# Attention into MoE on one core: a load goes ahead of another, and the third query chunk changes its score, turn and value paths

## The chip, the core and the metric

The kernel runs on one core of a Trainium2 chip. The metric is the device time of one execution in microseconds (us); lower is better. Before the change the median of three runs is 624.77 us.

The engines named below: TensorE (PE: matrix products; its weight loads, PEld, run beside it), VectorE (DVE), ScalarE (ACT), GpSimd (POOL) and SyncE (SP, which issues most transfers). PE writes into eight PSUM banks of 128 x 512 float32; ACT and DVE read them out.

## What is computed

Attention with a causal window of 128 and 4 sink positions, for 4 batches, 8 heads, 768 positions, head size 64, then a feed-forward layer (512 to 2048 to 512) with a leaky activation per column:

```python
keep = is_sink | in_window                  # pos < n_sink, or 0 <= q - k < window
scores = np.where(keep, scale * q @ k.T, -1e9)
a = softmax(scores); x = a @ v              # x: (3072, 512), heads side by side
h = x @ w_in
g = np.maximum(h, 0.0) + alpha * np.minimum(h, 0.0)
return g @ w_out
```

Inputs are float32; the feed-forward weights arrive as float64. To keep float32 accuracy the kernel splits a factor into a high and a low part of the format fp32r and adds three products (high x high, high x low, low x high), or it multiplies float32 directly.

## The kernel before

**Tiling.** The 3072 tokens are 12 chunks `c` of 256 queries, three to a batch (`CPB` = 3). For a chunk, attention makes x (512 features as 4 blocks of 128, high part `xh` and low part `xl`); then for each of 16 weight blocks `f` of 128 hidden columns `gemm1` makes h (12 matmuls of 256 columns, line 984), ACT and DVE make g with its two parts (L993, L995, L999, L1000), and `gemm2` adds into two output banks (6 matmuls of 512 columns, L1037, L1039, L1040). From chunk 3 on some blocks serve two chunks at once.

**Attention of a chunk.** A unit is one head `h` and one half `u` of the queries. Its steps: scores on PE into a bank; the mask, the scaling and the row maximum on DVE (L662); exp with the row sum on ACT (L668); weights turned so that keys lie on partitions; products with v; x written out by ACT and DVE. The sinks' part is collected apart (`sink_step`) and multiplied with the sink rows of v (`vs`).

There are three ways in which chunks do this:
- Chunks 0 and 1 (`SPLIT`): `load_head` brings two heads in one transfer, head `h` in partitions 0 to 63 and head `h+1` in 64 to 127. The scores of both are float32 matmuls on half the rows each, with nothing prepared (L637). PE turns the weights (L687, L688), ACT copies them into `comb` tiles (L692), and the row sums divide after the value product (`av_split`, L882 to L906).
- Chunk 2: each head is loaded twice over the partitions; ACT and DVE make the high and low parts (`prep_head`, L608 to L612); two fp32r matmuls of 128 rows for a unit (L647, L648). DVE divides (L697 to L709), PE turns (L786), DVE multiplies with the two triangle masks `tri` (L790), and `av_two` does the value product in two halves of four heads (L859 for the sinks, L838).
- Chunks 3 to 11 (`c >= PAIRED`): scores as in chunk 2. The weights are turned by a 32 x 32 transpose on DVE (L800) and transfers to DRAM and back (`swap`, L803, L807); DVE multiplies with masks (`swapped`, L821, L824), and `av_four` does all eight heads with 64 x 64 quarters of PE (L944 for the sinks, then L938 twice with a drain between).

**Weights.** A block is loaded (L415), its float64 words are made into float32 by two DVE steps (L427, L429), its high part is cast by ACT (L435) and its low part subtracted by DVE (L438).

**The order.** The program isn't issued as written. `Plan` collects operations with an engine, an estimated cost, and what they read and write; `draw` simulates them once in Python and places on each engine, as it comes free, the waiting operation of the lowest rank among those that could start soonest. PE operations are ranked as they were written; others take the rank of their first consumer. The order so found is fixed. Where PE would idle in the first 60 us of the plan, `issue` puts in matmuls of no use on an idle bank (L1224, `fill`). Values of a kind (tiles or banks) are given out in the order in which they were asked for. SP's queue holds its transfers in this order; the first ones are ranked by hand with `then(...)` (lines 532 to 545): parameters, head pair 0, weight block 0, head pair 2, head pair 4, sink rows, head pair 6, v, weight blocks 1 to 3.

**Where chunk 2 stands.** The feed-forward work of chunks 0 and 1 is a list of 32 slots (`work`, lines 1161 to 1184). Attention of chunk 1 is put at slot 0, that of chunk 2 is spread over the last `LATE` = 11 slots; `convert(f + 2)` keeps the weight conversion two blocks ahead. At the end `judge` works out whether the inputs fit this program (limits on window, sinks, weights and scores); five of its DVE steps (L1141 to L1145) need only the parameters and can run at the start.

## Time and profile before

| | |
|---|---|
| median of 3 runs | 624.77 us (624.73 to 625.24) |
| profiled execution | 624.71 us |
| its span, first to last instruction | 623.2 us |
| outside the span | 1.5 us |
| busy: PE, DVE, ACT, POOL | 615.2, 508.8, 367.0, 34.6 us |
| granted TensorE clock | 1.00 of full speed throughout |

The busy time of PE holds matmuls of no use, and pipelined matmuls overlap in it, so 99% is not 99% useful. The chain of waits gives each matmul the time that it adds to the one before it, and is the view by which PE's work is costed here.

### The profile page before, as it was taken

What the parts mean: (1) busy time and instruction counts of PE and PEld (TensorE: products, weight loads), DVE (VectorE), ACT (ScalarE), POOL (GpSimd) and SP (SyncE); (2) the same over time, 40 slices, a digit from 0 to 9 for tenths busy, and PEclk for the clock granted to TensorE, in tenths of its full rate; (3) what the DMA queues carried; (4) which work ended last, traced back from release to release, by engine and by line L of the source; (5) the groups of instructions that cost most, each with busy time, mean ns of one, the idle gap of its engine ahead of it and who ended that gap; (6) DMA issues with size and microseconds to landing.
All of it is one profiled execution on the core that took longest, in us unless ns stands there. A gap on an engine that the chain in (4) does not pass through costs nothing.

```text
span 623.2 us, 13103 instructions
## 1 busy us (share of the span) xinstructions
PE 615.2 (99%) x4594; PEld 547.4 (88%) x4596; DVE 508.8 (82%) x1637; ACT 367.0 (59%) x963; POOL 34.6 (6%) x116
## 2 busy tenths in 40 slices
PE   8999999999999999999999999999999999999997
PEld 4678999989999999998988888898898898898896
DVE  7999999979999989989689789879879969933232
ACT  6887558748567367365366266266366456369232
POOL 3110000001000000010000000010000000000000
PEclk9999999999999999999999999999999999999999
DMA  8777812235544354544534444344344343310001
GB/s 313 273 280 265 290 55 65 94 97 170 157 128 162 115 160 129 174 129 130 160 102 128 124 138 128 109 149 144 107 129 137 102 153 104 111 36 0 1 36 37
DMA packets 64039, 82.89 MB, mean 133 GB/s; under 512 B 9824, under 2 KB 45152, under 8 KB 63968
## 3 DMA queue, kind: packets, MB, share of 16 engines
q1 hardware_dynamic: 60416, 69.04, 35.3%
q10 hardware_dynamic: 3552, 12.97, 5.7%
q8 instruction: 37, 0.61, 0.4%
q14 instruction: 34, 0.28, 0.1%
HBM read 65.05 MB, written 16.94 MB: 132 GB/s over the span
## 4 chain that ended last, share of the span: by engine, by line
PE 95%; DVE 2%; ACT 1%; issue 1%; DMA 0%; ACTq 0%
PE bank L984 40%; PE bank L1039 13%; PE bank L1037 13%; PE bank L1040 13%; PE bank L938 4%; PE bank L647 3%; PE bank L648 3%; PE bank L838 1%; PE bank L637 1%; PE bank L944 1%; PE bank L687 1%; ACT pt L668 1%; PE bank L688 0%; DVE w L438 0%; PE bank L1224 0%
## 5 line engine op out<-in xcount | busy, mean ns | idle before, releaser
L984 PE MATMUL bank<-xh,w 128*128 128x256 f32 (+1 forms) x1136 | 263.7, 314 | 0.5 <-DVE g L995 0.5
L984 PEld LDWEIGHTS bank<-xh,w 128*128 128x128 f32 x1136 | 192.8, 191 | 12.8 <-DVE g L995 1.0
L984 PE MATMUL bank<-xl,w 128*128 128x256 f32 (+1 forms) x568 | 177.2, 312 | 0.0
L1039 PE MATMUL bank<-w,gh 128*128 128x512 f32 x380 | 144.5, 380 | 0.0
L1040 PE MATMUL bank<-w,gh 128*128 128x512 f32 x380 | 144.2, 379 | 0.0
L993 ACT ACTIVATE g<-bank,param 128x256 f32<-128x256 f32 (+1 forms) x142 | 77.7, 548 | 102.7 <-PE bank L984 102.4
L1037 PE MATMUL bank<-w,gl 128*128 128x512 f32 x380 | 113.5, 381 | 0.0
L984 PEld LDWEIGHTS bank<-xl,w 128*128 128x128 f32 x568 | 108.5, 191 | 5.2
L999 ACT CAST gh<-g 128x256 fp32r<-128x256 f32 (+1 forms) x142 | 67.5, 479 | 67.0 <-DVE g L995 66.4
L668 ACT ACTIVATE pt<-pt,nm 128x260 f32<-128x260 f32 (+1 forms) x192 | 93.5, 488 | 17.3 <-DVE nm L662 15.5
L995 DVE TENSOR_TENSOR g<-bank,g 128x256 f32<-128x256 f32 (+1 forms) x142 | 72.0, 512 | 33.4 <-ACT g L993 32.4
L1000 DVE TENSOR_TENSOR gl<-g,gh 128x256 fp32r<-128x256 f32 (+1 forms) x142 | 72.5, 515 | 20.4 <-ACT gh L999 18.5
L662 DVE CUSTOM_DVE_ANT_0 pt<-bank,masks 128x260 f32<-128x260 f32 (+1 forms) x192 | 71.4, 402 | 14.7 <-PE bank L648 12.4
L1039 PEld LDWEIGHTS bank<-w,gh 128*128 128x128 f32 x380 | 72.1, 190 | 8.2
L1037 PEld LDWEIGHTS bank<-w,gl 128*128 128x128 f32 x380 | 71.0, 189 | 9.5 <-issue 0.2
L1040 PEld LDWEIGHTS bank<-w,gh 128*128 128x128 f32 x380 | 72.0, 189 | 8.3
L608 ACT CAST kq<-stage 128x392 fp32r<-128x392 f32 (+1 forms) x80 | 38.7, 484 | 28.2 <-PE bank L648 16.9
L713 POOL TENSOR_TENSOR sink<-pt,ri 128x8 f32<-128x8 f32 x80 | 20.3, 255 | 459.3 <-DVE ri L698 411.2
L610 DVE TENSOR_TENSOR kq<-stage,kq 64x392 fp32r<-64x392 f32 (+1 forms) x80 | 42.1, 527 | 3.6 <-ACT kq L608 1.3
L709 DVE CUSTOM_DVE_ANT_0 comb<-pt,ri 128x128 f32<-128x128 f32 x136 | 43.4, 343 | 0.6
L648 PE MATMUL bank<-kq 128*128 128x260 f32 (+1 forms) x160 | 41.5, 275 | 0.0
L647 PE MATMUL bank<-kq 128*128 128x260 f32 (+1 forms) x160 | 40.7, 277 | 0.0
(131 smaller groups left out, 710.2 us busy)
## 6 DMA issues: line engine op xcount, KB each, us to landing
stage<-qk SPq DMA_DIRECT2D x56, 324.0 KB, 2.8
wraw<-w ACTq DMA_DIRECT2D x12, 1023.5 KB, 5.6
swap<-comb SPq DMA_DIRECT2D x36, 256.0 KB, 2.4
stage<-qk SPq DMA_DIRECT2D x24, 292.0 KB, 2.7
out_dram<-ob SPq DMA_DIRECT2D x22, 256.0 KB, 2.7
wa<-swap SPq DMA_DIRECT2D x36, 128.0 KB, 2.8
comb<-swap SPq DMA_DIRECT2D x36, 128.0 KB, 2.9
v<-vq SPq DMA_DIRECT2D x24, 192.0 KB, 3.4
```

The lines of the kernel that those rows point to most:

```text
L647: nc.tensor.matmul(s[:, w0], qh()[:, qs], keys, start=True, stop=False)
L648: nc.tensor.matmul(s[:, w0], ql()[:, qs], keys, start=False, stop=True)
L662: o = op("DVE", dve(n), lambda: nc.vector.tensor_tensor_reduce(out=pt.at[:, u, w0], in0=s.at[:, w0], in1=masks[:, i, w0], scale=-0.125, sc ...
L668: op("ACT", exp(n), lambda: nc.scalar.activation(pt.at[:, u, w0], pt.at[:, u, w0], AF.Exp, bias=nm.at[:, h, u:u + 1], scale=-1.0, accum_ou ...
L984: nc.tensor.matmul(h(), fin.win(part, ks), moving(name, kt), start=(kt == 0 and m == 0), stop=(kt == KT - 1 and m == 2))
L993: op("ACT", act(width, True), lambda g=g, h=h, view=view, f=f: nc.scalar.activation(view(g), h(), AF.Copy, scale=alt[:, f:f + 1]), reads=[ ...
L995: op("DVE", dve(width), lambda g=g, h=h, view=view: nc.vector.tensor_tensor(view(g), h(), view(g), ALU.max), reads=[bk], writes=keys(g))
L999: op("ACT", cast(width), lambda g=g, gh=gh, view=view: nc.scalar.copy(view(gh), view(g)), reads=keys(g), writes=keys(gh))
L1000: op("DVE", dve(width), lambda g=g, gh=gh, gl=gl, view=view: nc.vector.tensor_tensor(view(gl), view(g), view(gh).bitcast(F32), ALU.subtrac ...
L1037: nc.tensor.matmul(o2[j].at, gl.at[:, i, js], fin.row(0), start=False, stop=(f == end))
L1039: nc.tensor.matmul(o2[j].at, gh.at[:, i, js], fin.row(0), start=(f == begin), stop=False)
L1040: nc.tensor.matmul(o2[j].at, gh.at[:, i, js], fin.row(1), start=False, stop=False)
```

## The change

- **Order of the first transfers.** Head pair 2 goes ahead of weight block 0. The plan now counts the parameters' bytes, takes 400 KB/us before 25 us and 250 KB/us after (290 KB/us before), and lets marked DVE operations and all POOL operations exclude each other (`locks`).
- **Start of DVE and POOL.** The memset of `zeros` goes from POOL to DVE. The sink count and window (`pv`) are summed in another order. The memset of `tri` waits for the last mask. All of `judge` is placed behind the operation written last before it.
- **Chunk 0.** The turned weights of heads 4 to 7 go into `v` tiles, not `comb` tiles.
- **Chunk 2.** Pair loads and float32 scores on half the rows, as in chunks 0 and 1 (`WHOLE`), one head's bank of kind `s`, the other's of kind `pa`; turning by transfers, masks and `av_four` as in chunks 3 to 11 (`PAIRED` = 2). `masks_in_order`, which rearranges `tri` by four transfers, comes with it, and a further set of sink rows is loaded (`vs_prep(B)`). Its steps are spread over the last 14 slots, with two empty ones ahead of the value product; `trans` on PE and `av_two` are gone.
- **Sinks behind the values.** In `av_four` of chunks that don't begin a batch (2, 4, 5, 7, 8, 10, 11) the four sink matmuls come after the values, as an operation of their own.
- **Conversion.** `convert` runs five blocks ahead where a group has two members.

```diff
 SPLIT = (0, 1)
-PAIRED = 3
+WHOLE = (0, 1, 2)
+PAIRED = 2
...
-LATE = 11
+REST = 2
+LATE = 14
...
-AFTER = (1, 2, 3, 4)
...
-    def op(self, engine, cost, run, reads=(), writes=(), tail=0.09, mode=None, nbytes=0, other=None, locks=False):
+    def op(self, engine, cost, run, reads=(), writes=(), tail=0.09, mode=None, nbytes=0, other=None, locks=None):
...
-        o.locks = locks
+        o.locks = engine == "POOL" if locks is None else locks
...
-                dma = max(dma, t + 1.5) + o.nbytes / 290e3
+                dma = max(dma, t + 1.5) + o.nbytes / (400e3 if t < 25 else 250e3)
...
-    op("POOL", 1.2, lambda: nc.gpsimd.memset(zeros.at, 0), writes=[zeros])
+    op("DVE", 0.9, lambda: nc.vector.memset(zeros.at, 0), writes=[zeros])
...
-        if c in SPLIT and h % 2:
+        if c in WHOLE and h % 2:
...
-    then(lambda: setup("SP", ISSUE, lambda: nc.sync.dma_start(param, par), (), ("param",)))
+    then(lambda: setup("SP", ISSUE, lambda: nc.sync.dma_start(param, par), (), ("param",), nbytes=4 * P * (4 + NF)))
     then(lambda: load_head(0, 0))
+    then(lambda: load_head(0, 2))
     then(lambda: load_weights(0, "SP"))
-    then(lambda: load_head(0, 2))
     then(lambda: load_head(0, 4))
     then(lambda: vs_prep(0))
     then(lambda: load_head(0, 6))
...
-    setup("DVE", 0.1, lambda: nc.vector.scalar_tensor_tensor(pv, hi, 4294967296.0, wrap, op0=ALU.mult, op1=ALU.add), ("pf", "wrap"), ("pv",))
-    setup("DVE", 0.1, lambda: nc.vector.tensor_tensor(pv, pv, lo, ALU.add), ("pf",), ("pv",))
+    setup("DVE", 0.1, lambda: nc.vector.scalar_tensor_tensor(pv, hi, 4294967296.0, lo, op0=ALU.mult, op1=ALU.add), ("pf",), ("pv",))
+    setup("DVE", 0.1, lambda: nc.vector.tensor_tensor(pv, pv, wrap, ALU.add), ("wrap",), ("pv",))
...
-    setup("POOL", 0.35, lambda: nc.gpsimd.memset(tri, 1.0), (), ("tri",))
+    setup("POOL", 0.35, lambda: nc.gpsimd.memset(tri, 1.0), ("masks2",), ("tri",))
...
-        if c in SPLIT:
+        if c in WHOLE:
...
-        if c in SPLIT:
+        if c in WHOLE:
             pair = (h, h + 1)
-            banks_ = [val("h" if c == 0 and u else "s") for _ in pair]
+            banks_ = [val("pa" if c == 2 and x > h else "h" if c == 0 and u else "s") for x in pair]
...
+        while c not in SPLIT and len(softened) > 1:
+            softened.pop(0).urge = o
...
-            t = val("comb")
             o = P if c % CPB == 0 else 0
-            op("ACT", cast(4 * P - o, True), lambda: nc.scalar.copy(t.at[:, o:], tp.at[:, o:]), reads=[tp], writes=[t],
-               other=("DVE", dve(4 * P - o), lambda: nc.vector.tensor_copy(t.at[:, o:], tp.at[:, o:])) if c == 0 else None)
-            wt.setdefault((c, h // 2), []).append(t)
+            lends = c == 0 and h >= 4
+            t = val("v" if lends else "comb")
+            turned_ = (lambda: t.at.rearrange("p a h d -> p (a h d)")) if lends else (lambda: t.at[:, o:])
+            op("ACT", cast(4 * P - o, True), lambda: nc.scalar.copy(turned_(), tp.at[:, o:]), reads=[tp], writes=[t],
+               other=("DVE", dve(4 * P - o), lambda: nc.vector.tensor_copy(turned_(), tp.at[:, o:])) if c == 0 else None)
+            wt.setdefault((c, h // 2), []).append((t, lambda cols: turned_()[:, cols.start - o:cols.stop - o]))
             return
...
     def trans(c, p):
         if c in SPLIT:
             return
-        if c >= PAIRED:
-            return swapped(c, p)
-        tp, cb, tt = val("o"), comb.pop((c, p)), val("wa")
-        full = lambda: tt.at.bitcast(F32).rearrange("p (j u l x) -> p j u l x", j=2, u=2, l=2)
-
-        def turn(j):
-            for u in range(2):
-                o = (2 * j + u) * P
-                nc.tensor.transpose(tp.at[:, o:o + P], cb.at[:, o:o + P], ident)
-        for j in range(2):
-            op("PE", 2 * TURN, lambda j=j: turn(j), reads=[(cb, (j, 0)), (cb, (j, 1))], writes=[(tp, j)], tail=T_TAIL)
-        for j in range(2):
...
-        turned[c, p] = t, whole
+        turned[c, p] = t, whole, wide
...
+        t, whole, wide = turned.pop((c, p))
+        if not wide and p % 2 == 0:
+            rests[c] = val("comb")
+        rest = t if wide else rests[c]
...
-    def av_two(c, g):
-        both = (2 * g, 2 * g + 1)
-        src, v, bk = [wt.pop((c, x)) for x in both], [vtile.pop((c, x)) for x in both], val("pa")
-        vt, st = vst[c // CPB], sinkT[c]
-        place = lambda n: bk.at[:, n * QC:(n + 1) * QC]
-
-        def all_values():
...
-        op("PE", 2 * mm(QC) + 2 * values_cost(c), all_values, reads=src + v + [vt, st], writes=[bk], tail=N_TAIL, mode="col")
...
-        vt, st = vst[c // CPB], sinkT[c]
+        vt, st = vst[B if c == PAIRED else c // CPB], sinkT[c]
...
         def all_values():
-            for x in every:
-                nc.tensor.matmul(place(x), vt.at[:, x * P:(x + 1) * P], st.at.rearrange("p (i u b) -> p u i b", u=2, i=4), start=x % 2 == 0, stop=False)
             quarters(True)
             nc.tensor.drain()
             quarters(False)
+
+        def sinks():
+            for x in (0, 2, 1, 3):
+                nc.tensor.matmul(place(x), vt.at[:, x * P:(x + 1) * P], st.at.rearrange("p (i u b) -> p u i b", u=2, i=4),
+                                 start=not last and x % 2 == 0, stop=last and x % 2 == 1)
         x1, x2 = begin_x(c, 0)
-        op("PE", 4 * mm(QC) + 0.5 + 4 * native(P) * (3 if c % CPB else 2.5), all_values, reads=src + v + [vt, st], writes=bks, tail=N_TAIL, mode="col")
+        last = c % CPB > 0
+        if not last:
+            op("PE", 4 * mm(QC), sinks, reads=[vt, st], writes=bks, tail=R_TAIL)
+        op("PE", 0.5 + 4 * native(P) * (3 if c % CPB else 2.5), all_values, reads=src + v, writes=bks, tail=N_TAIL, mode="col")
+        if last:
+            op("PE", 4 * mm(QC), sinks, reads=[vt, st], writes=bks, tail=R_TAIL)
...
-                    if h == 0 and c == PAIRED:
-                        masks_in_order()
                     if h == FIFTH and c and c % CPB == 0:
...
-        if c in SPLIT:
+        if c in WHOLE:
             def pair_step(h, u):
                 def run():
                     if u == 0:
+                        if h == 0 and c == PAIRED:
+                            masks_in_order()
+                        if h == 4 and c == PAIRED:
+                            vs_prep(B)
...
+                        if c and (h in (0, 2) or c not in SPLIT):
                             load_v(c, h // 2)
...
+            if c not in SPLIT:
+                for at, st in ((8, lambda: trans(c, 3)), (8, sk), (8, lambda: trans(c, 2)), (8, None), (7, lambda: trans(c, 1)), (5, lambda: trans(c, 0))):
+                    steps.insert(at, st)
+                return steps + [None] * REST + [lambda: av_four(c)]
...
-        b = [lambda x=x: trans(c, x) for x in range(KT)]
-        b.insert(2, lambda: av_two(c, 0))
-        b.append(lambda: av_two(c, 1))
-        steps += [None, sk]
-        for n, st in enumerate(b):
-            steps += [st, None] if n in AFTER else [st]
-        return steps
...
-        on = lambda run, reads, write: op("DVE", 0.11, run, reads=reads, writes=[write])
+        here = plan.ops[-1]
+
+        def on(run, reads, write):
+            plan.order_after(op("DVE", 0.11, run, reads=reads, writes=[write]), here)
...
-        convert(group[-1][1] + 2)
+        convert(group[-1][1] + (2 if len(group) == 1 else 5))
...
-    rows = vs.reshape(B, P, DM).copy()
+    rows = np.concatenate([vs.reshape(B, P, DM), vs[:1].reshape(1, P, DM)])
```

## Rows read from the trace of the kernel before

**Rows 1.** Busy time by stretch: stretch, its length, then busy time (instructions) of each engine
```profile
10.00:20.00 10.00, 9.95 (x64) 5.58 (x63) 8.86 (x32) 9.34 (x33) 1.57 (x4) 1.00 1.04 403
...
60.00:70.00 10.00, 10.00 (x70) 9.37 (x69) 9.87 (x16) 5.70 (x11) 0.00 (x0) 1.00 0.73 246
```

**Rows 2.** PE's waits: who waited for whom, total us, times, longest
```profile
PE bank L984 <- DVE g L995: 0.5, 1, 0.5
```

**Rows 3.** Groups of PE by line: the matmuls of no use; count, busy us, mean ns
```profile
L1224 PE MATMUL bank<-idle 128*128 128x512 bf16 x23 | 8.1, 458 | 1.3 <-DVE fm L589 1.2
```

**Rows 4.** Chain that ended last, first 7 us: start, us added, what
```profile
2.70 0.60 DVE pf L575
...
3.50 0.08 DVE lent L572
...
3.69 0.09 DVE lent L574
...
4.16 0.20 DVE lent L571
...
5.96 0.06 DVE bad L1144
6.02 0.20 DVE pt L662
```

**Rows 5.** Timeline of the start, several engines: start, us, what, [idle before and its end]
```profile
7.49 0.76 DVE L427 CAST wa<-wraw 128x1024 f16<-128x1024 bf16 x1 [0.28 <-DMA wraw<-w]
...
8.99 0.94 PE L637 MATMUL bank<-lent 64*128 64x132 f32 x8
...
26.92 0.69 DVE L906 TENSOR_TENSOR xl<-ob,xh 128x512 fp32r<-128x512 f32 x1
```

**Rows 6.** Timeline of ACT, 6 to 18 us
```profile
9.54 1.05 ACT L435 CAST w<-wa 128x1024 fp32r<-128x1024 f32 x1 [0.40 <-DVE wa L429]
...
17.71 0.48 ACT L692 COPY comb<-bank 128x384 f32<-128x384 f32 x1 [0.67 <-PE bank L688]
```

**Rows 7.** Chain, 38 to 60 us: a pair of float32 scores; the chain through DVE
```profile
39.08 0.64 PE bank L637 x4
39.72 0.87 PE bank L984 x6
...
52.46 0.56 DVE kq L610
```

**Rows 8.** Chain, 100 to 136 us: chunk 2's attention on PE
```profile
100.57 0.11 PE bank L647
...
121.63 0.44 PE bank L786 x4
122.06 1.34 PE bank L984 x12
...
125.22 0.24 PE bank L859 x2
...
127.34 1.54 PE bank L984 x12
...
129.53 0.22 PE bank L1039
```

**Rows 9.** Chain, 213 to 220 us: chunk 4's value product on PE
```profile
215.26 0.49 PE bank L944 x4
...
218.93 0.31 PE bank L647
```

**Rows 10.** Timeline of DVE, 158 to 182 us: the end of chunk 3's attention
```profile
164.44 0.71 DVE L800 STREAM_TRANSPOSE comb<-comb 128x512 f32<-128x512 f32 x1
...
172.69 1.77 DVE L824 TENSOR_TENSOR comb<-comb,tri 64x256 f32<-64x256 f32 x4
...
180.38 1.28 DVE L954 TENSOR_TENSOR xl<-bank,xh 128x512 fp32r<-128x512 f32 x2
```

**Rows 11.** Chain, 172 to 180 us: the scores behind chunk 3's value product
```profile
177.25 0.31 PE bank L647
```

More of the change, by code (lines that the diff above doesn't have):

```diff
@@ L516, in program, with setup @@
     V = {}
-    def setup(engine, cost, run, reads=(), writes=()):
+    def setup(engine, cost, run, reads=(), writes=(), nbytes=0):
+        locks = engine in ("POOL", "DVE")
         for x in (*reads, *writes):
             V.setdefault(x, held(x))
-        return op(engine, cost, run, reads=[V[x] for x in reads], writes=[V[x] for x in writes])
+        return op(engine, cost, run, reads=[V[x] for x in reads], writes=[V[x] for x in writes], nbytes=nbytes, locks=locks)
     def known(x):
@@ L637, in scores @@
                     nc.tensor.matmul(bk.at[:, w0], st.at[r, KC:][:, qs], st.at[r, :KC][:, kw], start=True, stop=True)
-            op("PE", 1.47 * native(n), scores, reads=used, writes=banks_, tail=N_TAIL, mode="row")
+            o = op("PE", 1.47 * native(n), scores, reads=used, writes=banks_, tail=N_TAIL, mode="row")
         else:
@@ L728, in sink_step @@
             op("DVE", 0.15, lambda: nc.vector.tensor_scalar(four(), sm.at[:, 4 * g:4 * g + 4], 1e-9, None, op0=ALU.add),
-               reads=[(sm, (h, u)) for h in heads for u in range(2)], writes=[r])
+               reads=[(sm, (h, u)) for h in heads for u in range(2)], writes=[r], locks=True)
             op("DVE", 0.16, lambda: nc.vector.reciprocal(four(), four()), writes=[r])
@@ L777, in trans @@
             return
[L778 to L793 removed]
+        return swapped(c, p)
     def swap(c, p):
@@ L837, in values @@
             for j in range(2):
-                nc.tensor.matmul(a[j * D:(j + 1) * D, os], v[:, blk, j], weights(j)[:, ws], start=False, stop=stop and n == len(sets) - 1)
+                nc.tensor.matmul(a[j * D:(j + 1) * D, os], v[:, blk, j], weights(j)(ws), start=False, stop=stop and n == len(sets) - 1)
     def values_cost(c):
@@ L849, in begin_x @@
         return xh[c], xl[c]
-    def av_two(c, g):
-        both = (2 * g, 2 * g + 1)
-        src, v, bk = [wt.pop((c, x)) for x in both], [vtile.pop((c, x)) for x in both], val("pa")
-        vt, st = vst[c // CPB], sinkT[c]
-        place = lambda n: bk.at[:, n * QC:(n + 1) * QC]
-        def all_values():
-            for n, x in enumerate(both):
-                nc.tensor.matmul(place(n), vt.at[:, x * P:(x + 1) * P], st.at, start=n == 0, stop=False)
-            for n in range(2):
-                values(c, v[n].at, lambda j: src[n].at.bitcast(F32)[:, j * 4 * P:(j + 1) * 4 * P], place(n), n == 1)
-        op("PE", 2 * mm(QC) + 2 * values_cost(c), all_values, reads=src + v + [vt, st], writes=[bk], tail=N_TAIL, mode="col")
-        x1, x2 = begin_x(c, 2 * g)
-        view = lambda: halves(bk.at)
-        keys = [(x1, x) for x in both], [(x2, x) for x in both]
-        op("ACT", cast(4 * P, True), lambda: nc.scalar.copy(x1.at[:, g], view()), reads=[bk], writes=keys[0])
-        if not g:
-            for x in both:
-                load_v(c, x + 2)
-        op("DVE", dve(4 * P), lambda: nc.vector.tensor_tensor(x2.at[:, g], view(), x1.at[:, g].bitcast(F32), ALU.subtract),
-           reads=[bk, *keys[0]], writes=keys[1])
     def av_split(c, g):
@@ L939, in quarters @@
                                 place(x)[j * D:(j + 1) * D, to:to + (P if wide else D)], v[x].at[rows, blk, j], what,
-                                start=False, stop=not first and n == 1 and turn == len(low) - 1)
+                                start=last and first and n == 0 and turn == 0, stop=not last and not first and n == 1 and turn == len(low) - 1)
         def all_values():
-            for x in every:
-                nc.tensor.matmul(place(x), vt.at[:, x * P:(x + 1) * P], st.at.rearrange("p (i u b) -> p u i b", u=2, i=4), start=x % 2 == 0, stop=False)
             quarters(True)
@@ L1069, in run @@
                     finish_head(c, h)
[L1070 to L1072 removed]
+                    if 1 <= h <= KT:
+                        load_v(c, h - 1)
             return run
         sk = lambda g=0: sink_step(c, g)
[L1076 removed]
+        if c in WHOLE:
             def pair_step(h, u):
@@ L1199, in program @@
     slots = [[] for _ in range(n)]
-    for c in range(PAIRED, NCHUNK):
+    for c in range(PAIRED + 1, NCHUNK):
         for x, todo in enumerate(attention(c)):
```

72 lines of the change are left out of this document (30 added, 42 removed).

## The prediction, before the run

> **What bounds the kernel now.** I read the busy time by stretch first, because a share over the whole span would hide the start. From 60 us on PE is busy 10.00 of 10 us, while DVE has 9.87 and ACT 5.70; between 10 and 20 us PE shows 9.95, but DVE has 8.86 and ACT 9.34 as well [rows 1]. Second I asked what that busy PE does: 23 matmuls of no use, 8.1 us by the profile, all early [rows 3]. So there are two regimes. In the first 28 us PE mostly waits for attention of chunk 0, and ACT and DVE together set its pace: x of chunk 0 is whole only when L906, begun at 26.92 and 0.69 long, is done, at 27.6 [rows 5]. After that PE is packed, and the list of its waits has one entry worth naming, 0.5 us for DVE's g [rows 2]; the chain before it runs through DVE, chunk 2's preparation of keys among it [rows 7]. From 28 us to the end a microsecond saved on another engine is worth nothing, and one added on PE is a microsecond. The reader is to price the change twice: its start by waits of ACT and DVE, its chunk 2 by PE's chain alone.
>
> **The start.** Parameters arrive at 2.70, and the first softmax step begins at 6.02 [rows 4]; the chain between lies on DVE. Three steps in it need no parameters (L572, L574, L571: 0.08 + 0.09 + 0.20 = 0.37 us). The plan before counts no bytes for the parameters, so it believes them early and puts these three behind them; with the bytes counted they can run while DVE still waits. The memset of 1024 elements goes into the same gap. DVE's time for it is not in the trace; I bound it by L427's 0.76 [rows 5] and L435's 1.05 [rows 6] for as many elements. DVE is free of needed work from about 1.2 to 2.70, so memset and three steps fill the gap; at the upper bound perhaps 0.1 spills. Four steps of the later verdict (L1141 to L1144, 0.06 to 0.07 each, the last one shown) take 0.25 us of the chain [rows 4] and go to the end, where PE alone sets the pace. So the first softmax step comes 0.37 + 0.25 = 0.6 us earlier.
>
> Pair 2's load passes weight block 0. At 403 GB/s [rows 1] its 260 KB take 0.65 us, so it lands before rather than behind the block, and the block some 0.65 us after today's 7.49. Pair 2's scores begin at 8.99 today [rows 5]; they could begin right behind pair 0's. The block's delay is covered: DVE and ACT have pair 2's eight softmax steps to do in that time; without that cover it would cost its 0.65 us. What pair 2 can fill are two waits of ACT: 0.40 us before L435 and 0.67 us before L692, which waited for transposes queued behind the first value product [rows 6]. I take both, 1.07 us, less certain for the second. The start then gains 0.6 + 1.07 = 1.7 us. Bounds: a loss of 0.6 (the block's delay stays on the path, nothing else shows), and a gain of 4.5, since a good part of the 8.1 us of idle-bank matmuls [rows 3] lies before any score can run. I stay near the low end, because ACT at 9.34 of 10 has nothing more to give. The v tiles lent to chunk 0's late heads hold back chunk 1's v loads on SP; these are used a chunk later, so I cost them at nothing; if stage loads behind them come late, the loss is within the 0.6.
>
> **The stall at 59 us.** Chunk 2's early preparation (L610 at 52.46, 0.56 us) [rows 7] disappears, and DVE can be that much ahead. I take back 0.5 [rows 2]; bounds 0 and 0.5.
>
> **Chunk 2 on PE.** Before: 16 units of two matmuls at 0.11, 3.5 us; 16 transposes at 0.44 for four, 1.8; two for the sinks, 0.2; twice the value product, 125.22 to 127.34 plus 0.20 that the next 12 matmuls take over their 1.34, 2 x 2.32 = 4.6 [rows 8]. Sum 10.1 us. After: eight float32 pairs as in chunk 1, 0.64 each, and 0.87 for six matmuls behind it that otherwise take half of 1.34, so 0.84 and together 6.7 [rows 7, 8]; one value product of quarters, 215.26 to 218.93 plus 0.31 - 0.11 for the switch back, 3.9 [rows 8, 9]. Sum 10.6. So chunk 2 costs PE **0.5 us more**, not less. Bounds: without the switches, 1.6 less (-1.1); with 0.20 on both sides of each pair, 1.6 more (+2.1). I take the middle, for it is what chunk 1's pairs show.
>
> [...] The rows give 0.64 us for two heads in float32, against 4 x 0.11 = 0.44 for the split form of the same two [rows 7, 8].
> [...]
>
> On ACT and DVE chunk 2 loses its preparation and its masks on PSUM and gains transposes and masks on SBUF (L800 0.71, four of L824's kind 1.77) [rows 10]; on SP it gains swaps and four small transfers for `tri`, and a POOL step for the extra sink rows. All of this lies beside packed PE work: nothing, unless the handoff to chunk 2's `gemm1` fails (below). Five more verdict steps at the end run beside eight slots of PE work: nothing.
>
> **Sinks behind the values.** The four matmuls cost 0.49 wherever they stand [rows 9]; the switch of PE's tiling moves with them, from the scores that follow to the sinks. PE doesn't wait on the sinks' transfer today [rows 2], so the six chunks above 2 gain nothing. Bounds: 0.2 either way for each, 1.2; I take 0.
>
> **The sum.** -1.7 - 0.5 + 0.5 = -1.7. The profiled execution took 624.71 with a span of 623.2, so it gives 623.0; the median, 624.77, stands 0.06 above that execution, which changes nothing.
>
> **Rivals.**
> *The start keeps its length.* ACT and DVE are both near full in the first 28 us; a first softmax 0.6 earlier may only meet the next wait earlier (the plan's order puts weight conversion before the last pair), and PE's extra 0.5 stays. For it: ACT's 9.34 and DVE's 8.86 at once [rows 1]. Against: these two waits of ACT [rows 6] have pair 2's lateness or order behind them. With start and stall gaining 0.5 in all: 624.71 - 0.5 + 0.5 = 624.7.
>
> *The start gives much more.* The better-ordered plan keeps ACT and DVE on what chunk 0 needs and leaves weight block 1 behind. Pair 6's late units and the order of L906 leave room; a gain of 3.7 instead of 1.7 gives 621.0. Against: chunk 0 needs the same ACT work, and ACT is nearly full.
>
> *The handoff to chunk 2 stalls: slower.* Its values now come as one product, in the last of 32 slots, behind a transpose, two transfers in a row and masks. In chunk 3 the time from the last L800 to the end of its masks is 164.44 to 174.46, 10.0 us, and xl is whole 17 us after that transpose, at 181.7 [rows 10]. In chunk 2 the last pair's scores stand some 5.6 slots before the value product, of 1.34 + 6 x 0.22 = 2.7 us each [rows 8], 15 us in which those 10 us and the softmax of two heads must pass: chunk 0's first pair takes from 6.02 [rows 4] to the wait of ACT that ends at 9.54 [rows 6], 3.1 us, and the division comes on top. There is hardly a margin. Behind the product PE has only the `gemm2` of two blocks, 2.6 us, and chunk 3's first scores; chunk 3 needed 4.4 us from the end of its product, at 177.25 [rows 11], to whole xl. With values in time that is a stall of up to 1.8; it decides when they are later than the slot by more than some 1.5, and with 3 late the stall is 4.8 in all. I price it at 3.4: 626.4. Against: chunk 2's score work lengthens the slots by some 5 us in all, the two empty steps are room, and chunk 3 shows no wait of PE.
>
> **How the numbers follow.** Forecast 623.0: 0.50, own range 622.0 to 624.2; start much better, 621.0: 0.17; start unchanged, 624.7: 0.17; handoff stalls, 626.4: 0.16. A measurement of this kernel tells 0.2%, 1.25 us, from no change: faster is below 623.5, slower above 626.0. Faster: 0.40 of the forecast's 0.50 and 0.17, 0.57. Slower: 0.13 of the stall and 0.02 of the unchanged start, 0.15. Same: 0.28. The range leaves out the best of the large gains and the worse half of the stalls: 620.9 to 625.6, 0.09 below and 0.11 above.
>
> **What would show it.** The start is right if the first L662 begins near 5.4 instead of 6.02, pair 2's scores follow pair 0's without a weight conversion between, ACT's two waits are gone, and L906's second run ends near 25.9 instead of 27.6. Chunk 2 is right if its eight L637 pairs add 0.64 each to the chain and the matmuls behind them 0.2. The stall is excluded if PE's waits show nothing between 120 and 145 us, and shown if PE waits there for masks or for xh and xl. The prediction is wrong at its root if matmuls of no use or waits of PE appear behind 30 us, since it takes PE to be packed there.

## The result and the profile after

The changed kernel takes **631.07 us** (median of ten runs, 627.37 to 634.01) against 624.73 (624.62 to 625.24) for the kernel before, run beside it: ratio 1.0096, 95% interval 1.0076 to 1.0115. The forecast was 623.0, its range ended at 625.6, and it lies on the wrong side. The runs also spread over 6.6 us instead of 0.6. The profiled execution took 632.78 us, 1.7 above the median, with a span of 631.2, 8.0 more than the span of before.

**Where the 8.0 us are.** Four moments divide the span: the first and the last product of `gemm1` (from the listing of that line in each kernel: shortest, median and longest ns, then start of the first and the last in us), the start of the step that completes x of chunk 0 (`xl` of its second half on DVE), and the end.

```profile
L984 PE MATMUL bank<-xh,w x1136: 272/276/381, 20.2 to 613.4; 128*128 128x256 f32 x119, 128*128 128x512 f32 x71
L962 PE MATMUL bank<-xh,w x1136: 272/275/775, 22.6 to 620.5; 128*128 128x256 f32 x119, 128*128 128x512 f32 x71
```

| | first product | x of chunk 0 whole | last product | end of span |
|---|---|---|---|---|
| before | 20.2 | 26.92 | 613.4 | 623.2 |
| after | 22.6 | 32.75 | 620.5 | 631.2 |
| later by | 2.4 | 5.8 | 7.1 | 8.0 |

So 5.8 us are lost before x of chunk 0 is whole, 1.3 between there and the last product, 0.9 behind it. That the longest product of this kind takes 775 ns instead of 381 already says that TensorE ran slower for a while.

**The first 12 us.** DVE's order of time (start, busy, instruction, in brackets the idle time before it and what ended it):

```profile
5.28 0.30 DVE L664 CUSTOM_DVE_ANT_0 pt<-bank,masks 128x132 f32<-128x132 f32 x1 [0.58 <-PE bank L639]
...
6.50 0.42 DVE L664 CUSTOM_DVE_ANT_0 pt<-bank,masks 128x260 f32<-128x260 f32 x1
...
8.28 0.30 DVE L664 CUSTOM_DVE_ANT_0 pt<-bank,masks 128x132 f32<-128x132 f32 x1 [0.95 <-PE bank L639]
...
9.83 0.77 DVE L428 CAST wa<-wraw 128x1024 f16<-128x1024 bf16 x1 [1.25 <-DMA wraw<-w]
10.49 0.41 DVE L664 CUSTOM_DVE_ANT_0 pt<-bank,masks 128x260 f32<-128x260 f32 x1
```

The first softmax step begins at 5.28 instead of 6.02 [rows 4]: that part of the forecast came. But the conversion of weight block 0 (L428, the L427 of before) stands behind the first of pair 2's four steps on DVE and in front of the other three, and it waits until 9.83 for the block, which had landed by 7.49 in the kernel before [rows 5]. TensorE begins like this, after and then before:

```profile
1.22 2.74 PE L1202 MATMUL bank<-idle 128*128 128x512 bf16 x6 [1.22 <-DVE idle L1199]
4.44 1.68 PE L639 MATMUL bank<-lent 64*128 64x132 f32 x8 [0.48 <-DMA lent<-pairs]
6.05 1.46 PE L1202 MATMUL bank<-idle 128*128 128x512 bf16 x3
7.44 0.81 PE L639 MATMUL bank<-lent 64*128 64x132 f32 x4
...
1.23 3.17 PE L1224 MATMUL bank<-idle 128*128 128x512 bf16 x7 [1.23 <-DVE fm L589]
4.33 1.63 PE L637 MATMUL bank<-lent 64*128 64x132 f32 x8
5.89 0.82 PE L1224 MATMUL bank<-idle 128*128 128x512 bf16 x3
```

There are six matmuls of no use ahead of the first scores instead of seven, 0.48 us of idle time follows, and the next three take 1.46 us (0.49 each) where they took 0.82 (0.27 each). The first ones take 0.45 each in both kernels (2.74 for six, 3.17 for seven): TensorE starts at half its pace, and in the changed kernel it keeps that pace longer, until about 9.6 us instead of 5.8. The granted clock reads 1.00 in both stretches, so here the durations alone show the half pace.

**25 to 37 us.** ACT's order of time (ACTq is its queue, where it issues transfers):

```profile
23.84 0.38 ACTq L416 DMA_DIRECT2D wraw<-w  x1
...
24.93 0.20 ACT L670 ACTIVATION_READ_ACCUMULATOR pt<-pt,nm 128x1 f32 x1
29.20 0.38 ACTq L416 DMA_DIRECT2D wraw<-w  x1
29.68 0.59 ACT L855 COPY ob<-bank 128x512 f32<-128x512 f32 x1 [4.55 <-DMA tri<-trid]
...
11.93 1.17 SPq L774 DMA_DIRECT2D trid<-tri  x2
25.78 1.22 SPq L776 DMA_DIRECT2D tri<-trid  x2
...
SPq L776 <- DMA trid<-tri: 12.6, 1, 12.6
...
tri<-trid SPq DMA_DIRECT2D x2, 32.0 KB, 3.2
trid<-tri SPq DMA_DIRECT2D x2, 16.0 KB, 13.0
```

ACT does nothing from 25.13 to 29.68. Directly ahead of the step that is late, the copy of the row sums' inverse for x's second half, its queue holds the load of weight block 6, issued at 29.20, as the transfer `tri<-trid` lands. The lower rows say where that transfer comes from: `masks_in_order`. Its first two transfers (16 KB each) are issued at 11.93 on a queue whose weight blocks 1 to 3, of 1 MB each, have not landed yet (they land at 15.9, 18.5 and 23.2), and land 13.0 us later; SP waits 12.6 us for them before it can issue the other two. The first `tri<-trid` lands 3.4 us after its issue at 25.78, at 29.18, and ACT's load goes out at 29.20. Why the one waits for the other the trace doesn't show; that it does so is tried by e1 and e2 below.

The time by stretch (the columns are those of [rows 1]) shows what follows on TensorE:

```profile
28.00:29.00 1.00, 0.23 (x3) 0.04 (x1) 0.00 (x0) 0.00 (x0) 0.00 (x0) 1.00 0.98 191
29.00:30.00 1.00, 0.00 (x0) 0.00 (x0) 0.00 (x0) 0.32 (x1) 0.00 (x0) 1.00 0.95 363
30.00:31.00 1.00, 0.00 (x0) 0.00 (x0) 0.69 (x1) 1.00 (x2) 0.00 (x0) 0.50 0.89 199
31.00:32.00 1.00, 0.24 (x1) 0.24 (x2) 0.76 (x1) 1.00 (x4) 0.23 (x1) 0.50 0.82 187
...
35.00:36.00 1.00, 1.00 (x7) 1.00 (x6) 0.27 (x1) 0.00 (x0) 0.00 (x0) 0.50 0.44 169
36.00:37.00 1.00, 1.00 (x6) 0.78 (x7) 0.35 (x1) 0.86 (x2) 0.00 (x0) 0.59 0.02 8
37.00:38.00 1.00, 1.00 (x10) 0.66 (x9) 0.60 (x4) 0.60 (x2) 0.00 (x0) 1.00 0.00 0
```

It is idle from 28.2 to 31.7, the granted clock falls to 0.50 at 30.0, and TensorE works at that clock until 36.8.

These four transfers aren't new, as the prediction has it: the kernel before makes them for chunk 3, and two of them early as well.

```profile
16.88 1.31 SPq L770 DMA_DIRECT2D trid<-tri  x2
...
130.45 1.23 SPq L772 DMA_DIRECT2D tri<-trid  x2
```

There the other two, which write `tri`, had to wait until chunk 2's mask steps had read it. In the changed kernel chunk 2 uses the new order, nothing reads the old one, and so they run as early as the first two allow.

**Chunk 2 and the end.** A pair of chunk 2, the matmuls behind it, and the new stall in chunk 3:

```profile
121.36 0.71 PE L639 MATMUL bank<-stage 64*128 64x260 f32 x4
122.00 0.48 PE L1017 MATMUL bank<-w,gh 128*128 128x512 f32 x1
122.32 0.38 PE L1018 MATMUL bank<-w,gh 128*128 128x512 f32 x1
122.54 0.38 PE L1017 MATMUL bank<-w,gh 128*128 128x512 f32 x1
...
181.69 0.38 PE L962 MATMUL bank<-xh,w 128*128 128x256 f32 x1 [0.61 <-DVE g L973]
```

The pair takes 0.64 us and the next matmul 0.32 instead of 0.22. The value product with its sinks adds 3.84 us, from the end of the matmul ahead of it (136.33) to the next scores (140.17). The stall of 0.5 at 59 us [rows 2] is gone; one of 0.61 at 181.69 is new. And ACT's closing branch, before and after:

```profile
L1251 ACTq COMPARE_BRANCH  x1: 76/76/76, 620.5 to 620.5; - x1
L1251 ACTq EVENT_SEMAPHORE  x1: 17/17/17, 622.0 to 622.0; - x1
...
L1229 ACTq COMPARE_BRANCH  x1: 76/76/76, 627.4 to 627.4; - x1
L1229 ACTq EVENT_SEMAPHORE  x1: 17/17/17, 630.2 to 630.2; - x1
```

From the branch to the next instruction it takes 2.8 us instead of 1.5. In the changed kernel SP's closing wait is for ACT's branch, for 0.9 us behind the landing of the output; in the kernel before it has no such wait:

```profile
SPq L1404 <- ACTq L1229: 0.9, 1, 0.9
```

That is the loss behind the last product.

### The profile page after: what moved, and what is told of

The parts are those of the page before. It is cut to its first block, busy times and chain, and to the rows that moved or that the text cites. A ratio compares the mean times of both kernels' runs of the same rounds, so it can differ in the third digit from the quotient of the medians.

```text
span 631.2 us, 13257 instructions
## 1 busy us (share of the span) xinstructions
PE 618.6 (98%) x4660; PEld 546.3 (87%) x4660; DVE 509.0 (81%) x1635; ACT 361.2 (57%) x948; POOL 35.0 (6%) x116
## 5 line engine op out<-in xcount | busy, mean ns | idle before, releaser
L670 ACT ACTIVATE pt<-pt,nm 128x260 f32<-128x260 f32 (+1 forms) x192 | 93.5, 488 | 12.6 <-DVE nm L664 9.4
L610 ACT CAST kq<-stage 128x392 fp32r<-128x392 f32 (+1 forms) x72 | 34.6, 480 | 30.5 <-PE bank L650 18.9
L612 DVE TENSOR_TENSOR kq<-stage,kq 64x392 fp32r<-64x392 f32 (+1 forms) x72 | 38.3, 532 | 2.1
L650 PE MATMUL bank<-kq 128*128 128x260 f32 (+1 forms) x144 | 37.0, 274 | 0.0
L670 ACT ACTIVATION_READ_ACCUMULATOR pt<-pt,nm 128x1 f32 x192 | 36.3, 189 | 0.0
```

The lines of the kernel that those rows point to most:

```text
L612: op("DVE", dve(KC - n), lambda: nc.vector.tensor_tensor(ks()[D:, :, n // 2:], k_raw()[D:], ks()[D:, :, n // 2:].bitcast(F32), ALU.subtrac ...
L670: op("ACT", exp(n), lambda: nc.scalar.activation(pt.at[:, u, w0], pt.at[:, u, w0], AF.Exp, bias=nm.at[:, h, u:u + 1], scale=-1.0, accum_ou ...
```

## The experiments

Theory T: the early mask transfers hold ACT's queue, and the clock follows. Rival A: the load order and the late block 0 make the start late. Rival B: chunk 2 costs more than forecast. An edit that enters the plan makes `draw` choose a new order from there on (e1, e2, e3, e9, e11 to e15), which can move time elsewhere; an edit in what an operation runs leaves the order alone (e4; e5 against e1; e6; e8; e10 against e9; e16; e17).

| run | against the changed kernel | median, range (us) | first product | x whole | last product | ratio to before, 95% |
|---|---|---|---|---|---|---|
| e1 | mask transfers late | 628.18, 626.2 to 629.5 | 23.4 | 29.81 | 616.2 | 1.0035 to 1.0074 |
| e2 | mask transfers on POOL's queue | 628.91, 627.3 to 629.9 | 24.9 | 30.54 | 617.8 | 1.0042 to 1.0075 |
| e3 | pair 2 behind block 0 | 631.50, 626.3 to 633.2 | 20.9 | 31.32 | 619.4 | 1.0072 to 1.0129 |
| e4 | 16 fills in the stall | 630.76, 629.4 to 631.7 | 22.0 | 32.17 | 617.4 | 1.0085 to 1.0118 |
| e5 | e1 + 2 early fills | 626.30, 625.4 to 628.9 | 21.2 | 27.55 | 613.9 | 1.0016 to 1.0041 |
| e6 | *before*, 2 early fills less | 625.28, 624.5 to 626.0 | 20.8 | 27.60 | 614.1 | 0.9996 to 1.0015 |
| e8 | 2 early fills | 631.21, 629.7 to 633.3 | 24.0 | 34.21 | 621.1 | 1.0061 to 1.0119 |
| e9 | e1 + pair 2 behind block 0 | 625.68, 625.2 to 626.2 | 21.5 | 27.89 | 614.0 | 1.0003 to 1.0023 |
| e10 | e9 + 2 early fills + ACT's length | 624.41, 624.2 to 625.6 | 21.1 | 27.51 | 612.8 | 0.9987 to 1.0006 |
| e17 | e10, ACT's length 1019 | 624.06, 623.9 to 624.5 | 20.9 | 27.32 | 612.8 | 0.9977 to 0.9995 |

("Fills" are the matmuls of no use. The moments are those of one profiled execution; medians and moments need not agree, since the runs spread.)

**1. The mask transfers (e1, e2, e4).**

```diff
     def masks_in_order():
+        here = plan.ops[-1]
...
-            op("SP", ISSUE, lambda l=l: nc.sync.dma_start(trid.at[:, 1 - l], ...
+            o = op("SP", ISSUE, lambda l=l: nc.sync.dma_start(trid.at[:, 1 - l], ...
+            plan.order_after(o, here)
```

e1_masks_late. 

> The changed kernel with one edit: the four transfers that put the masks tri into block order are ordered behind the operation registered just before chunk 2, so that they run near 100 us instead of at 12 to 29 us. Theory T (these transfers hold SP, and ScalarE's queue waits for the landing of one of them before it may issue the load of weight block 6): ScalarE's 4.6 us of idle time before the copy of x's inverse at 29.7 us is gone, TensorE is not idle between 28 and 31.7, the granted clock stays at 1.0 from 30 to 37 us; 623.5 to 625, and the runs agree within 0.5 us instead of spreading over 6.6. Rival A (pair 2's load ahead of weight block 0 and the late conversion of that block cost the time): 629 or more. Rival B (chunk 2's new form costs more on TensorE than the 0.5 us forecast): 627 or more with the stall gone.

e2 issues the four transfers by GpSimd, as early as the plan allows (`op("POOL", ...)`, `nc.gpsimd.dma_start`). 

> [...] Theory T: as with the late transfers, 623.5 to 626 and no idle time of ScalarE behind a weight load near 29 us. If instead it is the early use of the transfer engines or of tri as such that costs, it stays at 629 or more.

```diff
                 def turn(u=u, o=o, both=both):
+                    for _ in range(16 if c == 1 and h == 0 and u == 0 else 0):
+                        fill(tp.at)
```

e4_fills. 

> The changed kernel with one edit: 16 matmuls of no use on the idle bank ahead of the transposes that TensorE waits with at 28 to 31.7 us, so that it is busy in the stall. Theory T: ScalarE's idle time stays, the clock stays at 1.0 behind it, and the time falls by the 3 us that the half clock costs: 627.5 to 628.5, with less spread. If the half clock has another cause than TensorE's idle time, it stays at 630 or more.

In e1 and e2 ACT's wait is gone and the clock holds from 25 to 35 us: e2's transposes at 29 to 31 us take 0.27 each, where the changed kernel's took 0.42 at 32. The first two rows are e1, the last two e4:

```profile
25.00:30.00 5.00, 5.00 (x44) 3.70 (x42) 4.97 (x10) 4.66 (x13) 1.17 (x2) 1.00 0.81 294
30.00:35.00 5.00, 4.93 (x38) 3.91 (x37) 4.73 (x13) 4.45 (x13) 0.87 (x2) 1.00 1.05 398
...
30.00:32.00 2.00, 1.95 (x14) 1.34 (x15) 1.63 (x2) 2.00 (x6) 0.81 (x2) 1.00 0.89 281
32.00:34.00 2.00, 2.00 (x16) 1.54 (x15) 1.83 (x6) 1.81 (x6) 0.06 (x1) 1.00 0.95 346
```

So T holds for the stall. In e1 the transfers run at 53.4 and 93.9 us. In e2 GpSimd issues them, two run at 19.6 and 21.0 and one at 26.3, among ACT's loads, and ACT isn't stopped (TensorE waits for it 0.2 us at most): it isn't their early run as such that stops ACT, but their issue by SP at that place. What links ACT's load to them was not shown. Yet both came out near 628.5, not at 624: T explains 2 to 3 us of the medians, and the spread stays at 2.6 to 3.3. Rival B falls: from x whole to the last product e1 takes 586.4 us, as the kernel before (586.5), with waits of 1.1 and 0.6 in it; but one pair of chunk 1's scores with its transposes, about 1 us, stands ahead of this stretch in e1 and in it before, so the two aren't quite the same work. In e4 TensorE is busy in the stall, the last two rows show the clock at 1.00 behind it, and from x whole to the last product it needs 585.2 us instead of 587.75: the half clock costs 2.5 us there, half of the 5.0 from 31.8 to 36.8. Its median fell by 0.3 only, so for the whole time e4 is inconclusive; two of its four runs show a mean clock of 0.995 and 0.996, so that it fell elsewhere in them. The clock goes with the spread of the changed kernel too: its lowest run, 627.37, has a mean clock of 0.999, and the eight from 629.23 up have 0.993 to 0.997; in e3 the run of 626.28 has 0.999, the six others, 631.1 to 633.2, have 0.994 to 0.996.

**2. The start (e3, e9, e5, e6, e8, e11).** e3 puts `load_head(0, 2)` behind `load_weights(0, "SP")` again, e9 does the same on e1.

e3_pair_behind. 

> The changed kernel with one edit: the load of chunk 0's second head pair goes behind weight block 0 again. Theory T: the stall at 25 to 30 us stays, 629 to 632. Rival A (the load order costs the time): 626 or less.

e9_late_w0_second. 

> The kernel with the late mask transfers (e1_masks_late), and the load of chunk 0's second head pair behind weight block 0 again, as in the kernel before. Theory L (the block, third in line, lands at 8.4 to 10.9 us instead of 7, and VectorE waits for it in the middle of pair 2's softmax, so that how late it lands sets the start and the spread): VectorE's L428 runs at 7.0 with a wait under 0.4, first gemm1 product at 20.5 to 21.2 us, 625 to 626, runs within 1 us. Rival (the load order doesn't matter; what is left of e1's loss over the kernel before is TensorE's half pace at the start and the closing branch): 627.5 to 628.5, as e1_masks_late.

```diff
             def scores():
+                for _ in range(2 if c == 0 and h == 0 and u == 0 else 0):
+                    fill(banks_[0].at)
```

e5_late_warm (on e1). 

> The kernel with the late mask transfers (e1_masks_late), and two more matmuls of no use on the idle bank ahead of the first scores, so that TensorE has no idle time at 3.97 to 4.71 us before them. Theory W (that idle time keeps TensorE at half pace until 13 us in e1_masks_late, where a fill still takes 0.46 us, and this makes the first product of gemm1 come at 23.4 instead of 20.2 us): fills and transposes at full pace from 6 us on, first gemm1 product at 20.5 to 21.5, 625 to 626, runs within 1 us of each other. Rival O (the order of the early steps alone, pair 2's scores ahead of the first transposes, makes the start late): 628, as e1_masks_late.

e8_warm_only (on the changed kernel). 

> The changed kernel with the two more matmuls of no use ahead of the first scores alone; the mask transfers stay early. Theory W with theory T (the transfers' stall at 25 to 30 us) as two separate costs: 628 to 629, the stall still there, and what is gained against the changed kernel is about what e5_late_warm gains against e1_masks_late. Rival: the stall absorbs an earlier start (it ends when the transfer lands, at 29.2 us), and the time stays at 630 to 631.

e6 lets `issue` stop 1.1 instead of 0.2 us ahead of an operation due before 5 us, in the kernel before. 

> The kernel before, with two of the seven matmuls of no use ahead of its first scores left out, so that TensorE is idle for some 0.9 us before them. Theory W: the transposes and fills behind run at half pace for some microseconds, the first product of gemm1 moves from 20.2 us to 21.5 or later, 626 to 628, with a spread of over 1 us. Rival O: 624.5 to 625, as the kernel before.

e11 is e5 with block 0's conversion behind pair 4's softmax (`plan.order_after(first, last_soft[0, 5, 1])`). 

> e5_late_warm (late mask transfers, TensorE busy up to the first scores, pair 2's load ahead of weight block 0) with the conversion of weight block 0 ordered behind the softmax of pair 4 on VectorE. Theory L: VectorE no longer waits for the block among the softmax steps, the runs come within 1 us of each other, and the median falls below e5_late_warm's 626.3 to 624.5 to 625.8. Rival (the block is needed as early as it comes; the conversion only becomes late for the first product): first gemm1 product at 22 us or later, 626 or more.

e3 alone looks like a defence of the load order, and is none. In its trace the first product comes 1.7 us earlier and the last 1.1, but the stall stays, and ACT's load goes out at 27.8 there, 29.2 in the changed kernel and 30.7 in e8; the medians of e3 and e8 show no gain. Without the stall the order counts: e9 is 2.5 us below e1 and its runs lie within 1.0. Where block 0's load is third, L428 began at 8.43 to 10.88 in the traces (e11 aside, which orders it later), where it is second at 6.97 to 7.74. With the stall out of the way, the latest and the earliest of the first kind (e2, e5):

```profile
6.54 0.29 DVE L664 CUSTOM_DVE_ANT_0 pt<-bank,masks 128x132 f32<-128x132 f32 x1
...
10.88 0.75 DVE L428 CAST wa<-wraw 128x1024 f16<-128x1024 bf16 x1 [4.05 <-DMA wraw<-w]
...
PE bank L639 <- DVE wa L428: 2.7, 1, 2.7
...
8.43 0.75 DVE L428 CAST wa<-wraw 128x1024 f16<-128x1024 bf16 x1 [1.09 <-DMA wraw<-w]
```

TensorE then waits 2.7 us in e2, and its granted clock was 0.76 between 12 and 16 us. That one block's landing moves by 2.5 us between the traces of these kernels, with DVE standing in front of it, is the likeliest source of the spread beside the clock; each kernel has one trace here, and what moves the landing stays open. TensorE's early idle time counts as well: e5 is 1.9 us below e1 with the same order. In the kernel before (e6) a gap of 0.62 us kept TensorE at half pace longer (three fills in 1.46 us again), with a first product 0.6 later and 0.6 us in the median, which its interval doesn't separate from nothing; expected were 626 to 628, 1.3 to 3.3 more. e11 (626.42, 625.4 to 627.8) gained nothing: DVE no longer waits for the block, but TensorE waits 1.8 us for pair 4's load, which also lies behind it. So DVE's order alone was not the cause; the landings behind the block count too.

**3. The plan's price of a transfer (e12, e13).** 400 KB/us before 25 us replaced by the old 290:

```diff
-                dma = max(dma, t + 1.5) + o.nbytes / (400e3 if t < 25 else 250e3)
+                dma = max(dma, t + 1.5) + o.nbytes / (290e3 if t < 25 else 250e3)
```

e12_rate. 

> The changed kernel with one number put back: the plan counts a transfer of the first 25 us at 290 instead of 400 GB/s. Theory R (the plan believes transfers landed too early; that is why VectorE waits for weight block 0 and ScalarE for vs among pair 2's softmax, and why the first scores have six matmuls of no use ahead of them instead of seven): no wait of VectorE on the block over 0.5 us, runs within 1.5 us of each other. The mask transfers stay early, but in another order, with another load of ScalarE behind each of them; if they still hold ScalarE's queue, 628 to 630, if not, 624.5 to 626. Rival (the load order alone makes the start late): 630 to 632 and the spread of the changed kernel.

e13_late_rate (on e1). 

> The kernel with the late mask transfers (e1_masks_late) and the old price of a transfer in the plan. Theory R: first gemm1 product at 20.5 to 21.5 instead of 23.4 us with pair 2's load still ahead of weight block 0, 625 to 626 with ScalarE's closing branch at 2.7 us (624 to 625 with 1.5), runs within 1.5 us. Rival (load order): 627.5 to 628.5 as e1_masks_late.

e12 came to 628.46 (627.5 to 629.8), e13 to 629.86 (628.1 to 633.3). The theory falls. The seventh fill is back, but L428 still waits 1.56 and 1.06 us for block 0, so the price isn't why it stands there. In e12 neither ACT's wait nor the half clock is there (1.00 from 25 to 35 us), but that adds little to T: in its redrawn order only the first mask transfer is early (12.9 us), the others run at 28.2, 32.3 and 38.2. e13 has the earliest first product of all, 18.9 us, and loses it at chunk 3's scores between 130 and 140 us, where its order lets TensorE stand for the row maxima of the scores before:

```profile
PE bank L649 <- DVE nm L664: 2.4, 3, 1.2
```

**4. The closing branch (e7, e10, e16).** e7 is e5 with `EARLIER = 30.0`, which puts the hint for the branch later. 

> e5_late_warm with the hints for the closing branch placed 30 instead of 85 us ahead of the planned end (EARLIER), so that fewer instructions lie between hint and branch. If the hint's place is why ScalarE's closing branch takes 2.7 us in the changed kernel against 1.5 us before (its event behind the branch at 630.2 against the branch at 627.4): 1.5 us there, and 0.9 us below e5_late_warm. If it is not: 2.7 us and the same time as e5_late_warm.

e10 is e9 with the two early fills and 13 copies of one element on ACT at 300 us; e16 is the kernel before with 10 such copies. 

> e9_late_w0_second with two more edits: the two matmuls of no use ahead of the first scores (TensorE not idle before them), and 13 copies of one element on ScalarE at 300 us, which make its program as many instructions long as in the kernel before (1011). If the place of the closing branch in ScalarE's program is why it takes 2.7 us instead of 1.5: 1.5 here. With theory W at 0.6 us (what the gap cost in e6_before_gap) and 0.9 us for the branch: 1.0 to 1.6 us below e9_late_w0_second, 623.8 to 624.6. If the length of ScalarE's program has nothing to do with it: 2.7 us there, 0.3 to 0.7 us below.

e16_before_pads. 

> The kernel before with 10 copies of one element added on ScalarE at 300 us, where it is half idle (its program 1019 instead of 1011 instructions long). If the place of the closing branch in ScalarE's program sets how long it takes, as the shorter programs of 989 to 1003 instructions with 2.7 us against 1.4 at 1011 suggest, it may take 2.7 us here too, and the time is 625.6 to 626.0; if only shorter programs are slow there, or the place doesn't matter, 1.4 to 1.5 us and 624.5 to 625.0.

The hint isn't it: e7 still needs 2.7 us (626.91, 626.4 to 628.7; its profile has L428 at 10.42). The length is. With ACT's program 989 to 1003 instructions long (1003 in the changed kernel), the event behind the branch came 2.6 to 2.9 us after it in every trace; with 1011, as before, 1.4 to 1.5; with 1019 it came in 0.6. e10 and e16:

```profile
L1238 ACTq COMPARE_BRANCH  x1: 76/76/76, 620.0 to 620.0; - x1
L1238 ACTq EVENT_SEMAPHORE  x1: 17/17/17, 621.4 to 621.4; - x1
...
L1256 ACTq COMPARE_BRANCH  x1: 76/76/76, 620.1 to 620.1; - x1
L1256 ACTq EVENT_SEMAPHORE  x1: 17/17/17, 620.7 to 620.7; - x1
```

e16 took 624.35 (624.2 to 624.9; ratio 0.9986 to 1.0004): less than the kernel before and not separated from it, where slower or equal had been expected. But a shorter branch shortens the end only as long as SP waits for it. From the branch to the end of the span it is 3.8 us in the changed kernel, 3.0 in e10 and e17 alike, and 2.7 in the kernel before and e16 alike: the step from 1.4 to 0.6 buys nothing. Already at 1.5, in the kernel before, SP waits for the output's landing (1.1 us) and not for ACT. What e16 has less in its trace (0.4 us of span) lies ahead of the branch, where ACT's last two copies wait 0.78 instead of 1.10 us; the kernel before, then e16:

```profile
619.27 0.65 ACT L1026 COPY ob<-bank 128x256 f32<-128x256 f32 x2 [1.10 <-PEq L1251]
...
618.90 0.65 ACT L1027 COPY ob<-bank 128x256 f32<-128x256 f32 x2 [0.78 <-PEq L1256]
```

The same 0.3 parts e17 from e10. e10 lies 1.3 below e9, in sum as expected from branch and fills together; in the traces 1.2 of it come ahead of the last product and 0.3 behind it.

**5. What is left of the gain (e14, e15, e17).** e14 is e13 with the old load order and ACT's length 1011, e15 is e10 with ACT's cast of `vs` behind pair 2's exps, e17 is e10 with 21 copies.

e14_late_rate_w0_second. 

> e13_late_rate with the load order of the kernel before as well, and 15 copies of one element on ScalarE at 300 us, so that its program is again 1011 instructions long and the closing branch takes 1.4 to 1.5 us. All four places of the loss are taken away. If the forecast's gains at the start (first softmax 0.6 us earlier) are real beside the old plan: 623.5 to 624.4. If the start's gains are lost to the next wait: 624.4 to 625, as the kernel before.

e15_vs_behind. 

> e10_late_w0_second_warm with ScalarE's cast of vs ordered behind the exps of pair 2 (and 15 instead of 13 copies of one element, so that ScalarE's program is again 1011 instructions long). If the in-order wait for vs's landing (1.05 us) is what keeps the start from gaining: no wait on vs, first gemm1 product at 20.0 to 20.6 us, 623.4 to 624.2, below the kernel before. If the start is bound elsewhere: first product near 21 and 624.3 to 624.8.

e17_all_mended. 

> e10_late_w0_second_warm with 21 instead of 13 copies of one element on ScalarE, so that its program is 1019 instructions long, where e16_before_pads had its closing branch done in 0.6 us instead of 1.4. If that carries over: 0.6 us at the branch, 623.5 to 624.0, below the kernel before by about 0.15%. If the branch's time depends on something else than the length: 1.4 us or more and 624.2 to 624.6.

e14 took 626.05 (625.6 to 626.5), e15 627.18 (626.7 to 629.5). e15 removes the wait of ACT for `vs` that e10's trace names (1.1 us). Both are slower than e10, since the redrawn order loses more elsewhere: from 130 us on TensorE waits 1.0 us for g and 0.7 for a later chunk's masks (at 306 us) in e15, 0.7 for g and 0.7 for chunk 4's sinks in e14, and 0.6 in all in e10. **e17 lies below both kernels**: 624.06, 0.14% (0.05 to 0.23) below the kernel before. Some 0.3 of that is ACT's earlier last copies, which the kernel before gets as well by the same length (e16, 624.35). The first product is still 0.7 later than before (20.9), although the first softmax begins earlier. The 1.7 us forecast at the start never came: the earliest whole x of all variants, in e14, is 0.6 earlier than before (26.36), and e14 loses it again.

## Why the prediction was wrong, step by step

- **"All of this lies beside packed PE work: nothing".** This failed first. The four small transfers of `masks_in_order` were costed as work of chunk 2, at 130 us. They have no producer but `tri`, and once chunk 2 no longer uses the old order nothing holds the last two back, so the plan put them at 11.93 and 25.78, and what they cost lies in another engine's queue. The prediction costed them at nothing and didn't ask when they become ready, nor who waits for their landing. Moving them gives back 2 to 3 us in the medians (e2, e1), and 5.1 from the first to the last product in e1's trace (597.9 against 592.8).
- **"It takes PE to be packed" behind 28 us.** The step named as the root was wrong: 28.2 to 31.7 idle, then half clock.
- **"The block's delay is covered."** The price was taken as 0.65 us, from the bytes ahead of it, with pair 2's eight softmax steps as cover. In the trace the conversion lies in front of six of them (three on DVE and the exps that follow them on ACT), and the block came 2.3 us later than before, not 0.65. The bound of 0.6 for a loss was the mis-sized term: e9 against e1 is 2.5.
- **ACT's two waits, 1.07 us.** Not regained: in their place ACT waits 0.90 us before pair 2's first exp, 1.02 before a copy of turned weights and 0.54 for `vs`.
- **First softmax 0.6 earlier.** Right: 0.74. It was worth nothing, since what follows waits for transfers; the rival "the start keeps its length" described this best, with too little loss.
- **Chunk 2 on PE, 0.5 us more.** Right in its terms: pairs 0.64, the matmuls ahead of and behind a pair 0.09 and 0.10 longer (0.20 forecast), value product and sinks 3.84 of 3.9 forecast. The net 0.5 itself isn't shown, since the stretches compared don't hold quite the same work; nothing in them says more.
- **The stall at 59 us, 0.5 back.** It is gone, but one of 0.61 at 181.69 is new: nothing gained.
- **Sinks behind the values at 0.** Nearly, in the changed kernel: TensorE's weight load waits 0.3 us for the sinks' transfer in chunk 4 (at 225.5). In e1 it is 1.1, far over the bound of 0.2 for a chunk, and before there was no such wait:

```profile
221.40 0.74 PE L921 MATMUL bank<-sinkT,vs 128*128 128x256 f32 x4 [1.14 <-DMA sinkT<-turns]
```

- **The handoff stall.** Excluded by the prediction's own sign: the changed kernel's TensorE shows no wait between 120 and 145 us. In e13 it stands there for 2.4 us, but for the row maxima of chunk 3's own scores, not for masks or x.
- **Not in the sum at all:** the early fill that fell out, and the closing branch (0.9). The v tiles lent to chunk 0's heads were costed at nothing; no run tried them alone.

In medians the way back is 631.07, 628.18 (transfers late, e1), 625.68 (load order, e9), 624.41 (fills and branch, e10), 624.06 (e17). What parts the last from the forecast of 623.0 is about the gain of the start that never came.

## What to carry over

When an edit moves a registration, ask of each of its operations when it becomes ready, not when its result is needed: a scheduler will run it as soon as it can, and a small transfer early is a small transfer behind the big ones (16 KB took 13.0 us here). Follow each transfer to whatever goes on only with its landing, on every engine: here ACT did nothing for 4.55 us, until a transfer that SP had issued was there. And before crediting a microsecond saved on a chain, look for the next in-order wait on a landing: a second cause (here the load order) stays hidden as long as another landing sets the end.

## What the runs showed of the hardware

- TensorE's first matmuls ran at half pace in every trace (fills at 0.45 us each) while the granted clock read 1.00. In the traces with 0.48 to 0.75 us of idle time ahead of the first scores (the changed kernel, e6, e1) fills still took 0.46 to 0.49 behind them, and full pace (0.27 or less) came at 9.6 to 13 us; in the others, with 0.35 or less there, it came between 4.1 and 7 us.
- The closing branch of ACT takes 0.6, 1.4 to 1.5 or 2.6 to 2.9 us with 1019, 1011 or 989 to 1003 instructions in ACT's program. The runs show that the length matters, not why, and that below 1.5 us the end no longer follows it.
- One block's landing differed by up to 2.5 us between traces of kernels that issue it at the same time (2.43 to 2.45 us), with transfers of the same bytes in front.
- A transfer of 16 KB landed 13.0 us after its issue behind large ones on SP's queue (the changed kernel), and 6.5 us after it when issued at 53.4 us (e1).
